# Banded attention and a squared-ReLU MLP in one kernel: bias matmuls ahead of the scores, masks at the start, and loads released by a memset

## The chip, the core and the metric

The kernel runs on one core of one Trainium2 chip, in one launch. The metric is the time of an execution on the device in microseconds; a kernel's time is the median of several executions. Engines are named as the profile names them: PE is TensorE (matmuls; PEld its weight loads), DVE is VectorE, ACT is ScalarE, POOL is GpSimd, which here issues all loads that convert from float32 to bfloat16, and SP is SyncE, which here issues the stores and the transposes made by DMA.

## The reference

q, k and v are float32 of shape (4, 8, 768, 64): batch, heads, sequence, head width. The attention is banded with a few global keys, and has a bias that falls linearly with distance. Its output goes through an MLP with a squared ReLU.

```python
scores = scale * np.matmul(q, k.transpose(0, 1, 3, 2))
is_global = pos[None, :] < 8
is_local = (rel >= 0) & (rel < 96)
keep = is_global | is_local
dist = np.where(is_global & ~is_local, 96.0, np.abs(rel))
bias = -slopes[:, None, None] * dist[None, :, :]
scores = np.where(keep, scores + bias[None], -1000000000.0)
a = softmax(scores)                       # over the keys
x = (a @ v) -> rows of 8 * 64 = 512       # 3072 tokens
out = (np.maximum(x @ w_in, 0.0) ** 2) @ w_out   # w_in 512 x 2048, w_out 2048 x 512
```

## The kernel before, in words

**Tiles and blocks.** The 3072 tokens are 24 tiles of 128, six for each batch entry. A local band of 96 reaches from a tile into its own keys and into those of the tile before it, and nowhere else; the eight global keys are copied over rows of the left tile that the band never reaches (lines 522 to 530 for k, 593 to 599 for v). The first tile of a batch entry has no left tile. Two tiles make a block of 256 tokens, which is what the MLP works on.

**A tile's attention.** q and k of tile j are brought into the layout with the head width on partitions. For tiles below `JQK` = 6 TensorE does it (`tr`, line 376, then a copy out of PSUM, `emit_T`); for later tiles SP issues one transpose by DMA (`emit_dT`, line 400, to `qkT`). Then come the scores (`emit_sc`, line 435), the exponential on ScalarE (line 483), the product with a mask `E` on VectorE (line 508), the matmul with v (`po`, line 550, whose 65th column is the softmax's sum), and the division (`emit_norm`, lines 577 and 578) that gives the tile's rows `x`. `x` is transposed in turn: by TensorE for tiles below `JX` = 6 (`trx`, line 613), by a DMA of SP's for the others (line 637, to `xT`).

**Bias and masks.** `pb` holds distance and mask for one tile, computed at the start from an iota. Tiles from `NBIAS` = 3 on multiply by `E`, the exponential of `pb` times each head's slope: eight activations (line 313), given to the planner as ready at 14 us. Tiles 0 to 2 have no mask product: `emit_sc` adds their bias in PSUM with a matmul of `pb` against a scaled identity `sid` (line 447), after the score matmuls of the same group.

**The MLP.** A block has eight steps. A step's first half, `hT` (line 661, eight matmuls of 256 columns), needs the block's `xT` and one part of w_in (`win_0` to `win_7`). ScalarE takes the ReLU (line 682), VectorE the square `hs` (line 694), and the second half, `acc` (line 731, four matmuls of 512 columns), needs a part of w_out. After eight steps the two halves of the block are copied out of PSUM (`emit_o`) and stored.

**Loads.** POOL issues q, k and v of a tile and the weight parts in a written order, 38 loads for tiles 1 to 7 and the weights, tile 0's v among them; tile 0's q and k come in float32 from SP. Tiles from 6 on (`late`) use `NQ` = 2 buffers in turn for q and k (`slot`), so a tile's load waits for the transpose of the tile two before it.

**Order.** Nothing is ordered by the loops. Every operation is entered in a `Plan` with an estimated cost on each engine that can do it, what it depends on, and a due time (`key`). `Plan.run` then lets the operation with the least start plus 0.05 x key go first, keeps track of each engine's free time and of buffers (`takes`), and so writes one fixed order for each engine. `LAG` is the delay the planner assumes from an operation's end to its user on another engine. SP and POOL are engines of the plan too (`SP`, `POOLQ`), and `DMAQ` stands for the transfers.

Of the kernel before, what the change touches and what calls it, by code (L numbers as in the profile page):

```python
# [21 lines left out]
class Plan:  # L22
# [9 lines left out]
    LAG = {"PE": 0.25, "ACT": 0.15, "DVE": 0.12, "SP": 2.6, "POOLQ": 0.8, "DMAQ": 1.2, "DMA": 0.0}  # L32
# [67 lines left out]
def kernel(  # L100
# [37 lines left out]
    JQK, JX = 6, 6  # L138
    NQ, NKT = 2, 2 * TPB
# [33 lines left out]
    E_AT = 14.0  # L173
    NWARM = 8
    LEAD = 12
# [65 lines left out]
    for j in range(NFIRST + 2):  # L241
        nc.vector.memset(v_sb[j][:, :, D : D + 1], 1.0)
    load_part(0, 1)
    nc.gpsimd.iota(pbi, pattern=[[-P, 2], [-1, P]], base=0, channel_multiplier=1)  # L244
    issue[0] += 0.4
# [9 lines left out]
    nc.vector.tensor_scalar(ident32, pbi[:, 0, :], 0.0, None, op0=Alu.is_equal)  # L255
    nc.vector.tensor_scalar(ident, pbi[:, 0, :], 0.0, None, op0=Alu.is_equal)
# [7 lines left out]
    )  # L264
    nc.vector.tensor_tensor(out=pb, in0=pbt, in1=pbw, op=Alu.min)
    for h in range(H):
        nc.vector.tensor_scalar_mul(sid[h], ident, float(slopes[h] / scale))

    def emit_pb0(e):
        nc.vector.tensor_copy(pb0, pb[:, 0, :])  # L270
        nc.vector.tensor_scalar_max(
            pb0[:n_global, :], pb0[:n_global, :], float(-n_local)
        )
        nc.vector.memset(pb[:n_global, 1, :], float(-n_local))

    pb_op = plan.op(("pb",), {"DVE": 0.75}, emit_pb0, key=-40.0)

    def emit_ones(e, js):
        for j in js:
            nc.vector.memset(v_sb[j][:, :, D : D + 1], 1.0)  # L280
# [22 lines left out]
    def any_copy(e, dst, src):  # L303
        if e == "ACT":
            nc.scalar.copy(dst, src)  # L305
        else:
            nc.vector.tensor_copy(dst, src)  # L307

    maskE = [
        plan.op(  # L310
            ("E", odd, g), {"ACT": 0.8}, key=0.3 + 2 * g + odd, ready=E_AT,
            emit=lambda e, odd=odd, g=g: [
                nc.scalar.activation(
                    E[:, odd, g, i], pb, Act.Exp, scale=float(slopes[4 * g + 2 * i + odd])
                )
                for i in range(2)
            ],
        )
        for g in range(2)
        for odd in range(2)  # L320
    ]

    def emit_E0(e, odd):
# [8 lines left out]
            ("E0", odd), {"DVE": 0.6}, emit=lambda e, odd=odd: emit_E0(e, odd), key=9 + odd,  # L332
            deps=[maskE[odd], maskE[2 + odd]],
# [7 lines left out]
    xT_op = {}  # L341
    xT_of = {}
# [3 lines left out]
    for j in range(NT):  # L346
# [6 lines left out]
        if j in late:  # L353
            def emit_load(e, j=j):
                load_tile(j)
            ld = plan.op(
                ("load", j), {"POOLQ": 2.6}, emit_load, deps=qk_users[slot(j)] + [ones[j]],
                key=base, ready=issue[0],
            )
            qk_users[slot(j)] = []  # L360
            ld = plan.op(("data", j), {"DMAQ": 2.7}, None, deps=[ld], key=base)
            land["q", j] = land["k", j] = land["v", j] = ld
# [6 lines left out]
        for n in range(2) if j < JQK else ():  # L369
            users = []  # L370

            def emit_tr(e, j=j, n=n, fp=fp):
                tr = ps_g.tile([P, NPAIR, P], FP32 if fp else BF16, name="tr", tag="g")
                src = plain[n, j] if fp else qk_ring[slot(j)][:, n, :]
                for pair in range(NPAIR):
                    nc.tensor.transpose(  # L376
                        out=tr[:, pair, :], in_=src[:, pair * P : (pair + 1) * P],
                        identity=ident32 if fp else ident,
                    )
                tiles["tr", n, j] = tr  # L380

            tr = plan.op(
                ("tr", n, j), {"PE": 0.5 if fp else 0.24}, emit_tr,
                deps=[land["qk"[n], j]], key=base, takes=(*G, [users]),
            )

            def emit_T(e, j=j, n=n, T_=T_):
                any_copy(e, T_[:, n], tiles.pop(("tr", n, j)))

            c = plan.op(  # L390
                ("T", n, j), {"DVE": 0.7 if fp else 0.43, "ACT": 0.57}, emit_T,
                deps=[tr] + ku, key=base + 0.1,
            )
            users += [tr, c]
            parts.append(c)
            if not fp:
                qk_users[slot(j)].append(tr)
        if j >= JQK:
            def emit_dT(e, j=j, T_=T_):
                nc.sync.dma_start_transpose(  # L400
                    out=T_.rearrange("p n a c -> p (n a) c"),
                    in_=qk_ring[slot(j)].rearrange("p n c -> p (n c)"),
                )

            T = plan.op(
                ("T", j), {"SP": 2.0}, emit_dT,
                deps=[land["q", j], land["k", j], xT_op[j - 3]] + ku, key=base - 6,
            )
            qk_users[slot(j)].append(T)
            parts = [T]  # L410
# [8 lines left out]
        def emit_sc(e, gs, j=j, first=first):  # L419
            sc = {}  # L420
            for g in gs:
                for odd in range(2):
                    sc[odd, g] = ps_g.tile([P, 4, P], FP32, name="sc", tag="g")
                    tiles["sc", j, odd, g] = sc[odd, g]
            todo = [
# [4 lines left out]
            todo = [x for x in todo if x[0] in gs]  # L430
            opened = set()
            for g, pair, at, kt in todo:
                for odd in range(2):
                    half = slice(odd * D, (odd + 1) * D)
                    nc.tensor.matmul(  # L435
                        out=sc[odd, g][:, at, :],
                        lhsT=qkT[(j - kt) % NKT][half, 1, pair, :],
                        rhs=qkT[j % NKT][half, 0, pair, :],

                        start=j >= NBIAS or (odd, g) not in opened,  # L440
                        stop=j >= NBIAS,
                        skip_group_check=True,
                    )
                    opened.add((odd, g))
            for g, pair, at, kt in todo if j < NBIAS else ():
                for odd in range(2):
                    nc.tensor.matmul(
                        out=sc[odd, g][:, at, :],
                        lhsT=sid[2 * pair + odd],
                        rhs=pb0 if first else pb[:, kt, :],  # L450
                        start=False,
                        stop=True,
                        skip_group_check=True,
                    )

        deps = list(parts)
        if j < NBIAS:
            deps.append(pb_op)
# [3 lines left out]
        for gs in [(0,), (1,)] if j < NSPLIT and not first else [tuple(range(groups))]:  # L462
            n = 8 * len(gs)
            o = plan.op(
                ("sc", j, gs[0]), {"PE": 0.25 + 0.029 * n + (0.056 * n if j < NBIAS else 0)},
                lambda e, gs=gs, f=emit_sc: f(e, gs), deps=deps, key=base + 1 + 2 * gs[0],
                takes=(*G, busers[2 * gs[0] : 2 * gs[-1] + 2]),
            )
            ku.append(o)
# [3 lines left out]
        for g in range(groups):  # L473
            for odd in range(2):
# [3 lines left out]
                def emit_exp(e, j=j, odd=odd, g=g):  # L478
# [11 lines left out]
                    ("exp", j, odd, g), {"ACT": 0.58}, emit_exp, deps=[s_[g]],  # L490
# [3 lines left out]
                users += [s_[g], x_]  # L494
# [6 lines left out]
                def emit_mul(e, j=j, odd=odd, g=g, first=first):  # L501
# [10 lines left out]
                    ("mul", j, odd, g), vec(0.38), emit_mul,  # L512
                    deps=[x_, maskE0[odd] if first else maskE[2 * g + odd]],
# [8 lines left out]
        if 1 <= t < TPB - 1:  # L522
            def emit_gk(e, j=j, t=t):
# [5 lines left out]
                ("gk", j), vec(0.17), emit_gk, deps=list(s_.values()), key=base + 4  # L529
# [7 lines left out]
        for hf in range(2):  # L537
# [34 lines left out]
            def emit_norm(e, j=j, hf=hf):  # L572
# [13 lines left out]
                ("norm", j, hf), vec(0.6), emit_norm,  # L586
# [6 lines left out]
        if 1 <= t < TPB - 1:  # L593
            def emit_gv(e, j=j, t=t):
# [3 lines left out]
                ("gv", j), vec(0.28), emit_gv, deps=[p_, norm[1]], key=base + 5  # L598
# [7 lines left out]
        if j < JX:  # L606
# [23 lines left out]
            c = plan.op(("xT", j), {"DVE": 0.43, "ACT": 0.57}, emit_xT, deps=[f_], key=base + 5.1, takes=xT_ring)  # L630
            users += [f_, c]
            xusers.append(f_)
        else:
# [8 lines left out]
            c = plan.op(("xT", j), {"SP": 1.3}, emit_xT, deps=norm, key=base + 5, takes=xT_ring)  # L642
# [4 lines left out]
        if tt == 1:  # L647
            c["deps"].append(xT_op[j - 1])
# [5 lines left out]
    for n, (blk, s) in enumerate(order1):  # L654
# [31 lines left out]
        r = plan.op(("relu", blk, s), {"ACT": 0.58}, emit_relu, deps=[a], key=n + 0.5, takes=("hr", 2, [rusers]))  # L686
# [10 lines left out]
        d = plan.op(("sq", blk, s), vec(0.68), emit_sq, deps=[r], key=n + 1.0, takes=("hs", NHS, [husers]))  # L697
# [11 lines left out]
    for blk in range(NBLK):  # L709
# [9 lines left out]
        for s, sub, half in order2:  # L719
# [29 lines left out]
            if s == NSTEP - 1:  # L749
                ousers = []  # L750

                def emit_o(e, blk=blk, sub=sub, half=half, cols=cols):
                    o_sb = work.tile([P, d_model], FP32, name="o", tag="o", bufs=4)
# [4 lines left out]
                    ("o", blk, sub), {"ACT": 0.57, "DVE": 0.62} if half is None else {"ACT": 0.37},  # L758
                    emit_o, deps=[o], key=8 * blk + s + 1.0, takes=("o", 4, [ousers]),
# [4 lines left out]
                def emit_st(e, blk=blk, sub=sub, half=half, cols=cols):  # L764
# [5 lines left out]

                st = plan.op(
                    ("st", blk, sub), {"SP": 0.4}, emit_st, deps=[ev],
                    key=8 * blk + s + 9.0,
                )
                ousers.append(st)

    for o in plan.run({"PE": 4.2, "DVE": 4.4, "ACT": 4.2, "DMAQ": issue[1]}):
# [37 lines left out]
```

## Time and profile before

| what | value |
|---|---|
| time, median of 4 | 216.16 us (215.95 to 216.53) |
| the profiled execution's own time | 215.99 us |
| its span, first to last instruction | 213.9 us |
| granted TensorE clock | 1.000 |
| PE / PEld busy | 206.7 us (97%) / 142.0 us (66%) |
| DVE / ACT busy | 141.2 us (66%) / 118.7 us (55%) |
| DMA queue of POOL's loads | 13.37 MB, 79200 packets |
| DMA queue of SP | 13.90 MB, 34480 packets |
| chain that ended last | PE 86%, DMA 7%, POOL 4% |

The profile is of one execution. Its span leaves out 2.1 us of the time of the same execution around it. Busy time of PE counts each matmul from its start to its modelled end; matmuls overlap, so a group of eight with 273 ns each takes 0.87 us. Where the profile puts an idle stretch down to a releaser, the wait for several semaphores is given to the one that came last.

### The profile page before, as it was taken

The page shows a single profiled execution, that of the slowest core. Times are in us where ns is not written, and L with a number is a line of the kernel's source. Part 1 is how long each engine was busy: PE and PEld are TensorE (multiplying, and loading weights), DVE is VectorE, ACT ScalarE, POOL GpSimd, SP SyncE. Part 2 cuts the span into 40 slices and gives each one's busy share as a digit, 9 for nine tenths or more (in the row PEclk, how much of TensorE's full clock was granted, in tenths as well). Part 3 has the DMA queues.
Part 4 walks back from the last instruction along what each step waited for, and adds up shares of the span by engine and source line. Part 5 has one row for each costly group of instructions (what it writes and reads, how often), then busy time and mean ns, then how long its engine had stood idle before and what let it go on. Part 6 is the DMA issues. An engine that isn't in the chain of part 4 may idle for free.

```text
span 213.9 us, 5031 instructions
## 1 busy us (share of the span) xinstructions
PE 206.7 (97%) x1992; PEld 142.0 (66%) x1992; DVE 141.2 (66%) x366; ACT 118.7 (55%) x218; POOL 74.1 (35%) x91
## 2 busy tenths in 40 slices
PE   7888999999999999999999999999999999999994
PEld 3666567657667767766767767766767767766773
DVE  5376968736688767756867767756867767744540
ACT  2587675714574845743845745743845745734431
POOL 7996677309044414309043140408113000000000
PEclk9999999999999999999999999999999999999999
DMA  9999999999999999999979959999989810310202
GB/s 129 145 160 197 181 196 181 178 220 112 158 196 127 218 99 124 159 136 100 198 101 104 212 71 111 149 126 96 204 128 91 175 25 3 123 25 3 98 0 98
DMA packets 113702, 27.58 MB, mean 129 GB/s; under 512 B 104336, under 2 KB 110736, under 8 KB 113680
## 3 DMA queue, kind: packets, MB, share of 16 engines
q0 software_dynamic: 79200, 13.37, 82.9%
q1 hardware_dynamic: 34480, 13.90, 34.0%
q8 instruction: 15, 0.25, 0.5%
q14 instruction: 7, 0.06, 0.1%
HBM read 27.26 MB, written 6.29 MB: 157 GB/s over the span
## 4 chain that ended last, share of the span: by engine, by line
PE 86%; DMA 7%; POOL 4%; issue 1%; DVE 0%; ACT 0%; POOLq 0%
PE hT L661 38%; PE acc L731 38%; PE sc L435 5%; PE po L550 5%; DMA win<-in_moe_w_in_dram 4%; DMA qk<-in_k_dram 3%; POOL qk L193 2%; POOL v L193 2%; POOL win L193 1%; PE tr L376 0%; PE trx L613 0%; DVE x L578 0%; ACT o L305 0%; POOL pbi L244 0%; DVE v L595 0%
## 5 line engine op out<-in xcount | busy, mean ns | idle before, releaser
L661 PE MATMUL hT<-xT,win 128*128 128x256 bf16 x768 | 99.0, 273 | 0.5 <-DMA win<-in_moe_w_in_dram 0.3
L731 PE MATMUL acc<-wout,hs 128*128 128x512 bf16 (+1 forms) x400 | 95.6, 370 | 0.0
L682 ACT ACTIVATE hr<-hT 128x512 f32<-128x512 f32 x96 | 57.3, 598 | 60.4 <-PE hT L661 58.9
L661 PEld LDWEIGHTS <-win 128*128 128x128 bf16 x768 | 71.0, 98 | 18.2 <-DMA win<-in_moe_w_in_dram 1.0
L694 DVE TENSOR_TENSOR hs<-hr 128x512 bf16<-128x512 f32 x96 | 65.0, 689 | 25.5 <-ACT hr L682 24.8
L731 PEld LDWEIGHTS <-hs 128*128 128x128 bf16 x400 | 38.4, 98 | 27.7 <-DVE hs L694 0.3
L483 ACT ACTIVATE esc<-sc 128x512 bf16<-128x512 f32 x78 | 42.6, 599 | 13.2 <-PE sc L435 13.1
L193 POOL DMA_DIRECT2D qk<-in_q_dram x23 | 20.6, 898 | 82.2 <-DMA qkT<-qk 79.7
L508 DVE TENSOR_TENSOR at<-esc,E 128x512 bf16<-128x512 bf16 x78 | 32.4, 420 | 6.9 <-ACT esc L483 5.8
L193 POOL DMA_DIRECT2D v<-in_v_dram x24 | 21.6, 902 | 2.4 <-DVE at L508 1.2
L578 DVE TENSOR_TENSOR x<-po,rs 128x256 bf16<-128x256 f32 x48 | 20.4, 424 | 1.7
L193 POOL DMA_DIRECT2D qk<-in_k_dram x23 | 20.7, 899 | 0.2 <-issue 0.2
L550 PEld LDWEIGHTS <-at 128*128 128x128 bf16 x352 | 16.7, 98 | 5.5
L550 PE MATMUL po<-v,at 128*128 128x65 bf16 x352 | 18.6, 193 | 0.0
L435 PEld LDWEIGHTS <-qkT 64*128 64x128 bf16 x352 | 9.9, 94 | 10.0 <-issue 8.3
L577 DVE RECIPROCAL rs<-po 128x4 f32<-128x4 f32 x48 | 8.6, 179 | 10.4 <-PE po L550 10.2
L435 PE MATMUL sc<-qkT 64*128 64x128 bf16 x192 | 13.2, 219 | 1.0 <-ACT qkT L305 0.5
L305 ACT COPY o<-acc 128x512 f32<-128x512 f32 (+1 forms) x14 | 7.8, 556 | 9.2 <-PE acc L731 9.2
L307 DVE COPY o<-acc 128x512 f32<-128x512 f32 x11 | 7.6, 691 | 6.2 <-PE acc L731 6.2
L435 PE MATMUL sc<-qkT,qkT 64*128 64x128 bf16 x160 | 11.4, 216 | 0.0
L524 DVE COPY qkT<-qkT 128x32 bf16<-128x32 bf16 x16 | 3.0, 189 | 7.5 <-PE sc L435 7.5
L193 POOL DMA_DIRECT2D win<-in_moe_w_in_dram x8 | 6.6, 822 | 0.9 <-DMA wout<-in_moe_w_out_dram 0.6
(40 smaller groups left out, 61.4 us busy)
## 6 DMA issues: line engine op xcount, KB each, us to landing
out_dram<-o SPq DMA_DIRECT2D x23, 256.0 KB, 3.3
v<-in_v_dram POOLq DMA_DIRECT2D x24, 128.0 KB, 6.2
qk<-in_q_dram POOLq DMA_DIRECT2D x23, 128.0 KB, 4.9
qk<-in_k_dram POOLq DMA_DIRECT2D x23, 128.0 KB, 5.6
win<-in_moe_w_in_dram POOLq DMA_DIRECT2D x8, 256.0 KB, 8.5
wout<-in_moe_w_out_dram POOLq DMA_DIRECT2D x8, 256.0 KB, 8.8
qkT<-qk SPq DMA_TRANSPOSE x18, 5.0
xT<-x SPq DMA_TRANSPOSE x18, 3.6
```

What stands on the lines that cost most here:

```text
L193: nc.gpsimd.dma_start(out=dst, in_=src)
L305: nc.scalar.copy(dst, src)
L435: nc.tensor.matmul(out=sc[odd, g][:, at, :], lhsT=qkT[(j - kt) % NKT][half, 1, pair, :], rhs=qkT[j % NKT][half, 0, pair, :],  start=j >= N ...
L483: nc.scalar.activation(out=esc, in_=tiles.pop(("sc", j, odd, g)).rearrange("p a c -> p (a c)"), func=Act.Exp, scale=scale,)
L508: nc.vector.tensor_mul(at, tiles.pop(("esc", j, odd, g)), bias)
L550: nc.tensor.matmul(out=po[:, hi, :], lhsT=tiles["at", j, odd, g][:, at * P : (at + 1) * P], rhs=v_sb[kj][:, h, :], start=(i == 0), stop=(i ...
L577: nc.vector.reciprocal(rs, po[:, :, D : D + 1])
L578: nc.vector.tensor_tensor(out=x[:, 4 * hf : 4 * hf + 4, :], in0=po[:, :, :D], in1=rs.to_broadcast([P, 4, D]), op=Alu.mult,)
L661: nc.tensor.matmul(out=hT[:, c, :], lhsT=w_in_sb[s][:, kt, c * P : (c + 1) * P], rhs=tiles["xT", blk][:, kt, :], start=(kt == 0), stop=(kt ...
L682: nc.scalar.activation(hr, tiles.pop(("hT", blk, s)), Act.Relu)
L694: nc.vector.tensor_mul(hs, hr, hr)
L731: nc.tensor.matmul(out=tiles["acc", blk, sub, half], lhsT=hs[:, c, sub * P : (sub + 1) * P], rhs=w_out_sb[s][:, c, cols], start=(s == 0 an ...
```

## The change

It has six parts.

1. The bias matmuls of tiles 0 to 2 become an operation of their own (`emit_bias`) that opens the PSUM group ahead of the score matmuls, and may be placed as soon as the tile's k is transposed by TensorE. The scores then close the group.
2. `pb` is finished at once at the start, and the eight `E` activations are issued there, outside the plan. The iota goes ahead of the first load on POOL.
3. From tile 8 on a load has a gate: a memset on VectorE of one element for each row and half of the buffer that the load will write. The load, which writes the same buffer, then waits for VectorE. In the plan the gate comes after the landing of the load before it, and after the issue of the `xT` transpose of the tile three before it.
4. There are three buffers for q and k of late tiles instead of two (`NQ`).
5. `JX` becomes 8: x of tiles 6 and 7 is transposed by TensorE.
6. The planner's costs and lags are changed (SP's lag from 2.6 to 0.6 with transfers as operations of their own on `DMAQ`; shorter costs on ACT and DVE), so the orders it writes change throughout. `NLATE` as set leaves the stores' dependencies as they were.

The diff, cut to its core:

```diff
-    LAG = {"PE": 0.25, "ACT": 0.15, "DVE": 0.12, "SP": 2.6, "POOLQ": 0.8, "DMAQ": 1.2, "DMA": 0.0}
+    LAG = {"PE": 0.25, "ACT": 0.26, "DVE": 0.2, "SP": 0.6, "POOLQ": 0.8, "DMAQ": 1.2, "DMA": 0.0}
...
-    JQK, JX = 6, 6
-    NQ, NKT = 2, 2 * TPB
+    JQK, JX = 6, 8
+    NQ, NKT = 3, 2 * TPB
...
-    E_AT = 14.0
     NWARM = 8
+    NLATE, NO = 2, 4
...
+    nc.gpsimd.iota(pbi, pattern=[[-P, 2], [-1, P]], base=0, channel_multiplier=1)
     load_part(0, 1)
-    nc.gpsimd.iota(pbi, pattern=[[-P, 2], [-1, P]], base=0, channel_multiplier=1)
-    issue[0] += 0.4
     load_part(1, 1)
...
+    nc.vector.tensor_copy(pb0, pb[:, 0, :])
+    nc.vector.memset(pb[:n_global, 1, :], float(-n_local))
+    nc.vector.tensor_scalar_max(pb0[:n_global, :], pb0[:n_global, :], float(-n_local))
     for h in range(H):
         nc.vector.tensor_scalar_mul(sid[h], ident, float(slopes[h] / scale))
...
+    for g in range(2):
+        for odd in range(2):
+            for i in range(2):
+                nc.scalar.activation(
+                    E[:, odd, g, i], pb, Act.Exp, scale=float(slopes[4 * g + 2 * i + odd])
+                )
...
+            gate = None
+            if j >= NFIRST + 2 + NQ - 1:
+
+                def emit_gate(e, j=j):
+                    nc.vector.memset(qk_ring[slot(j)][:, :, :1], 0.0)
+
+                gate = plan.op(
+                    ("gate", j), {"DVE": 0.07}, emit_gate, deps=qk_users[slot(j)] + [ld, xT_sp.get(j - 3)],
+                    key=base - 9,
+                )
             ld = plan.op(
-                ("load", j), {"POOLQ": 2.6}, emit_load, deps=qk_users[slot(j)] + [ones[j]],
-                key=base, ready=issue[0],
+                ("load", j), {"POOLQ": 2.6}, emit_load,
+                deps=qk_users[slot(j)] + [ones[j], gate], key=base, ready=issue[0],
             )
...
-                ("T", j), {"SP": 2.0}, emit_dT,
+                ("T", j), {"SP": 1.3}, emit_dT,
                 deps=[land["q", j], land["k", j], xT_op[j - 3]] + ku, key=base - 6,
             )
+            T = plan.op(("moved", j), {"DMAQ": 1.2}, None, deps=[T])
...
+        def emit_bias(e, gs, j=j, first=first, todo=todo, open_sc=open_sc):
+            open_sc(gs)
+            opened = set()
+            for g, pair, at, kt, odd in todo(gs):
+                nc.tensor.matmul(
+                    out=tiles["sc", j, odd, g][:, at, :],
+                    lhsT=sid[2 * pair + odd],
+                    rhs=pb0 if first else pb[:, kt, :],
+
+                    start=(odd, g) not in opened,
+                    stop=False,
+                    skip_group_check=True,
+                )
+                opened.add((odd, g))
...
+            if j < NBIAS:
+                bias = plan.op(
+                    ("bias", j, gs[0]), {"PE": 0.056 * n},
+                    lambda e, gs=gs, f=emit_bias: f(e, gs), deps=[tr],
+                    key=base + 0.9 + 2 * gs[0], takes=takes,
+                )
+                takes = None
             o = plan.op(
-                ("sc", j, gs[0]), {"PE": 0.25 + 0.029 * n + (0.056 * n if j < NBIAS else 0)},
-                lambda e, gs=gs, f=emit_sc: f(e, gs), deps=deps, key=base + 1 + 2 * gs[0],
-                takes=(*G, busers[2 * gs[0] : 2 * gs[-1] + 2]),
-            )
+                ("sc", j, gs[0]), {"PE": 0.2 + 0.029 * n},
+                lambda e, gs=gs, f=emit_sc: f(e, gs), deps=[*deps, bias],
+                key=base + 1 + 2 * gs[0], takes=takes,
+            )
...
-            c = plan.op(("xT", j), {"SP": 1.3}, emit_xT, deps=norm, key=base + 5, takes=xT_ring)
+            c = plan.op(("xT", j), {"SP": 1.2}, emit_xT, deps=norm, key=base + 5, takes=xT_ring)
+            xop = xT_sp[j] = c
+            c = plan.op(("xmoved", j), {"DMAQ": 0.9}, None, deps=[c])
             xusers.append(c)
...
-    for o in plan.run({"PE": 4.2, "DVE": 4.4, "ACT": 4.2, "DMAQ": issue[1]}):
+    for o in plan.run({"PE": 4.2, "DVE": 4.2, "ACT": 5.3, "DMAQ": issue[1]}):
```

In the orders that the plan writes for the changed kernel, `win`, `wout` and the tiles' loads stand on POOL as before; on SP the transpose of tile 6 stands ahead of the first store, and from tile 10 on each tile's `qkT` transpose stands behind the `xT` transpose of an earlier tile; 16 gate memsets stand among VectorE's squares and products.

## The prediction

> **What bounds the kernel now.** I read the page's busy rows and slices first, then the busy time by stretches, then TensorE's own timeline of the first 30 us, and last the rows on the transfers.
>
> ```profile
> PE 206.7 (97%) x1992; PEld 142.0 (66%) x1992; DVE 141.2 (66%) x366; ACT 118.7 (55%) x218; POOL 74.1 (35%) x91
> PE   7888999999999999999999999999999999999994
> PEclk9999999999999999999999999999999999999999
> ```
>
> ```profile
> 10.00:20.00 10.00, 8.75 (x137) 6.97 (x135) 6.27 (x38) 8.10 (x19) 8.28 (x11) 1.00 1.86 173
> 20.00:30.00 10.00, 9.25 (x100) 5.89 (x99) 8.07 (x22) 7.01 (x15) 7.54 (x10) 1.00 1.62 189
> 30.00:45.00 15.00, 15.00 (x146) 10.11 (x144) 11.41 (x27) 9.27 (x18) 7.28 (x9) 1.00 1.85 182
> 45.00:100.00 55.00, 55.00 (x526) 37.32 (x524) 37.82 (x90) 30.13 (x54) 21.88 (x25) 1.00 1.39 149
> ```
>
> The columns of the stretches are length, busy time of PE, PEld, DVE, ACT, POOL, clock, DMA share, GB/s. TensorE is busy without a gap from 30 us on, at full clock; time can only be gained before that, or by giving it less work. Busy time hides part of the gaps because ends of matmuls overlap, so I took starts: a matmul should start after its predecessor by 0.056 us (128 columns), 0.109 (256), 0.2155 (512) or 0.029 (65), the usual step in the trace. What exceeds this after 5 us is 5.40 us: 1.15 before 10 us, 2.28 from 10 to 20, 1.68 from 20 to 30, 0.29 later. Where:
>
> ```profile
> 7.17 0.40 PE L435 MATMUL sc<-qkT 64*128 64x128 bf16 x8 [0.37 <-ACT qkT L305]
> 11.73 0.40 PE L376 MATMUL tr<-ident,qk 128*128 128x128 bf16 x4 [0.21 <-DMA qk<-in_q_dram]
> 17.18 0.40 PE L376 MATMUL tr<-ident,qk 128*128 128x128 bf16 x4 [0.62 <-DMA qk<-in_k_dram]
> 24.47 1.05 PE L661 MATMUL hT<-xT,win 128*128 128x256 bf16 x8 [0.32 <-DMA win<-in_moe_w_in_dram]
> 27.45 0.40 PE L376 MATMUL tr<-ident,qk 128*128 128x128 bf16 x4 [0.22 <-DMA qk<-in_k_dram]
> 28.00 1.05 PE L661 MATMUL hT<-xT,win 128*128 128x256 bf16 x8
> ```
>
> Most of these wait for a load to land. The 38 loads of the first 40 us follow each other at 0.87 us (q, k, v) and 1.3 us (weights), so their landings are rails that no order of TensorE's moves: q and k of tile 2 at 11.68 and 12.51, win_1 15.02, k of tile 3 17.14, win_2 19.23, wout_0 20.50, win_3 21.80, wout_1 23.08, win_4 24.42, win_5 29.61 (semaphore events of the trace). The question is what else TensorE has ready at each rail.
>
> **The change part by part.** I followed the changed kernel's queues in their written order, with these durations and landings; ScalarE's 512-column operations follow each other at 0.48 us, VectorE's copy takes 0.42.
>
> *Constants.* The iota goes ahead of the first load on POOL: that load issues 0.37 us later (the iota's row), the second at the same place, so the other rails stay. VectorE's pb chain starts at 1.59 and is done at 3.66. Masks: eight activations at 0.306 each (four in 1.33 us at 13.47) run from 3.70 to 6.27 in ScalarE's idle 3.44 us there, and 2.5 us leave its queue at 13.5, 19.5 and 22.6. Cover: k of tile 0 wants ScalarE at 6.56, so 0.3 us spare; beyond that it costs one for one, up to the 1.1 us that tile 1 waits for q of tile 2.
>
> *Bias ahead.* Same 40 matmuls. Tile 0's eight (0.45 us) stand in the gap of 0.44 us before 7.17; its first exponential starts at 7.74 instead of 8.10, tile 0's first po at 8.95 instead of 9.65. Then both versions stand at the rails 11.68 and 12.51. After 12.60: transposes 0.23, bias 0.45, trx 0.22, bias 0.54, scores 0.55: the first step of the MLP (hT) at 14.59, against 15.30. win_1 is in at 15.02, so the second follows at 15.47; before, it stood behind k of tile 3, at 17.66. At 17.46 TensorE is thus one hT step (0.87) and one po group (0.24) ahead. The scores of tile 3 come at 18.18 and 18.95 (before 19.05 and 21.61). The rails 19.23 to 24.42 hold both versions (before: 19.38, 20.64, 21.94, 23.12, 24.47); between them the new order finishes tile 3: last po 22.77 (25.35), trx 23.99 (26.85), its xT copied at 25.0 (27.94).
>
> *The gain.* So block 1's steps may start at 25.39 instead of 28.00. Before win_5 lands, three of them fit (25.39, 27.34, 28.44) where one did; the other work up to there is the same. Two steps of 8 x 0.109 = 1.74, and win_5's step starts at 29.96 instead of 29.66: 1.74 - 0.30 = 1.44 us ahead. From 30 to 45 us the old gaps of 0.29 go and one of 0.35 appears (wout_7 landing at 40.09, its acc step now due at 39.8): -0.06.
>
> *x of tiles 6 and 7 by TensorE.* Eight transposes at 0.056: +0.45 us on the bound engine, nothing hides it. The two DMA transposes removed saved nothing: the tighter one landed 0.10 us before its use at 68.23. Its PSUM copies (0.41 on VectorE or 0.48 on ScalarE) lie beside matmuls.
>
> *Gates and third buffer.* 16 memsets of a few elements; nearest row 65 ns for 128x8: 1.0 us of VectorE, idle a third of the time. Should one have to wait, squares (hs) queue behind it and acc behind them. Four gates name a transpose that VectorE hasn't waited for yet; the earliest, at about 54.3, needs the one issued at 43.0, some 6 us done. Bounds: 0, and where a transpose took 9 us, still 2 us spare; I take 0. POOL's three loads per tile stay behind the gate, not beyond what the score needs: the first gated load issues earlier (45.7, before 48.6), as the third buffer is free.
>
> The cost is elsewhere. In SP's queue each qkT transpose now stands one tile period (8.04 us) nearer to its scores: 6.6 to 8.6 us from issue to use in the steady part, before 14.4 to 16.6.
>
> ```profile
> L400 SPq DMA_TRANSPOSE qkT<-qk x18: 1232/1290/2596, 43.0 to 167.8; - x18
> ...
> DMA to landing us min/median/max: 3.1/5.0/9.0
> ...
> POOL qk L193 <- DMA qkT<-qk: 79.7, 13, 9.1
> ```
>
> Landing took 3.1 us with nothing else moving (issue 158.42) and 9.03 with three loads and two stores under way (135.81). The Trainium skill's Advanced Engine Details and Errata, section X-Bar Transpose (TRN2), has it that transposes by DMA are as fast as regular DMAs, at an expected 350 to 400 GB/s. That speaks against gating: 256 KB in 0.7 us would never miss 6.6 us, the gates would buy nothing and the sum stays -0.93. By the row, at the old latencies and a budget of 7.3, the three slowest (7.6, 8.3, 9.0) exceed it by 3.0 us together, 2.5 us for the 15 transposes of the steady part: the sum would be +1.6. I take the row, but not its upper end: the gates issue the loads mostly 0.7 to 3 us after the transpose, so it starts in front of them, and only the overlap is slow. Between 140.5 and 142 us, with both moving, the transpose got about 0.4 of its lone rate: 1 us of transfer becomes 2.5 at worst, 3.1 + 1.5 = 4.6, and a store ahead adds 0.7 each: 6.0. Below 6.6, so 0; ends 0 and +2.5. A gain below 0 is excluded, since the scores were never late after 50 us.
>
> *The sum.* -1.44 + 0.06 + 0.45 = -0.93 us on the profiled execution (span 213.9, its own time 215.99): span 213.0, own time 215.06. That execution is 0.17 below the median 216.16, so the median becomes 215.2.
>
> **The rivals.**
> (1) Transposes come late, slower than before. Place: the scores at the head of each tile, every 8.04 us from 60 to 173. Price above: +2.5 - 0.93, about 217.7. It decides once the misses total 0.93 us; two transposes at the old maximum suffice. For: the budget is halved. Against: loads and transposes no longer start together.
> (2) The startup yields one step, not two. ScalarE has two relu operations ahead of k of tile 3 at 17.32, and tile 3's scores wait for that copy; if its chain slips by 1 us, only two steps of block 1 fit before win_5: 0.87 - 0.30 - 0.06 - 0.45 = 0.06 gained, 216.1: no change. Against: tile 3 has 1.9 us more than before for the same queue.
> (3) More gain: the wait at 40.14 and the 0.30 at win_5 don't appear: 0.93 + 0.65, 214.6. For: the landing of the last weights varies with the stores near it.
> That the gates hold nothing back is possible too; then the queue is as before with less budget, which is rival 1.
>
> **How the numbers follow.** Forecast 0.52 (215.2, alone 214.9 to 215.6), rival 3 0.14, rival 2 0.12, rival 1 0.22. Differences under 0.2%, 0.43 us, can't be told from none here. Faster: 0.52 + 0.14 + some of rival 2's better half (0.03) = 0.69; same 0.11, with small misses of rival 1; slower 0.20. The range 214.4 to 217.3 leaves out rival 1's upper part and the tail of rival 3.
>
> **What would show it.** In the profile after: E activations on ACT before 6.5 us; hT at about 14.6 and 15.5 on TensorE, and three hT steps of block 1 before the one that waits for win_5; trx x32 instead of x24; most POOL loads issued 0.7 us or more after a qkT transpose, not just ahead of it, and a median landing of qkT near 3.5 to 4.5. Wrong: idle time of PEld before L449 (scores) put down to a DMA qkT after 50 us, VectorE idle before the memset L346, or a tile period above 8.1 us; or block 1's first step still near 28.

## The result, and the profile after

The changed kernel takes 215.66 us (median of 43 runs, 214.49 to 217.35); the kernel before 216.21 (64 runs). The ratio is 0.9973, 95% interval 0.9961 to 0.9986: faster by 0.27%, a little more than this kernel's measurement can tell from no change. The forecast was 215.2 us, 0.9956 of the 216.16 it started from. In a second group of runs it was 215.26 against 216.16, ratio 0.9932 (0.9901 to 0.9962): the forecast's ratio lies between the two. The profiled execution was a lucky one: its own time is 214.53 with a span of 212.8, where the median span of its group is 213.5; before it was 215.99 and 213.9.

The busy row and the slice of TensorE from the page of after:

```profile
PE 205.2 (96%) x2000; PEld 141.7 (67%) x2000; DVE 143.2 (67%) x384; ACT 118.2 (56%) x218; POOL 74.4 (35%) x91
PE   6978999999999999999999999999999999999993
```

Its busy time by stretches (columns as before):

```profile
10.00:20.00 10.00, 8.01 (x122) 6.48 (x121) 6.65 (x39) 6.73 (x15) 8.69 (x12) 1.00 1.84 174
20.00:30.00 10.00, 9.43 (x99) 6.73 (x98) 6.40 (x17) 5.63 (x11) 7.30 (x10) 1.00 1.63 189
45.00:100.00 55.00, 55.00 (x524) 36.78 (x522) 37.38 (x97) 28.78 (x52) 18.43 (x21) 1.00 1.23 137
```

From 45 us on TensorE is still busy without a gap, so the steady part lost nothing to waits. From 10 to 20 us it is busy for less time than before (8.01 against 8.75): part of its work there was done earlier, and the same loads hold it up. The gain shows in TensorE's timeline:

```profile
12.52 0.40 PE L372 MATMUL tr<-ident,qk 128*128 128x128 bf16 x4 [0.45 <-DMA qk<-in_k_dram]
14.52 1.92 PE L675 MATMUL hT<-xT,win 128*128 128x256 bf16 x16
17.97 0.23 PE L449 MATMUL sc<-qkT 64*128 64x128 bf16 x2 [0.55 <-ACT qkT L304]
24.35 1.92 PE L675 MATMUL hT<-xT,win 128*128 128x256 bf16 x16
27.20 1.04 PE L675 MATMUL hT<-xT,win 128*128 128x256 bf16 x8
28.29 1.04 PE L675 MATMUL hT<-xT,win 128*128 128x256 bf16 x8
29.82 1.92 PE L675 MATMUL hT<-xT,win 128*128 128x256 bf16 x16
```

The group at 14.52 is two steps of the MLP, 14.52 and 15.40. The one at 24.35 is win_4's step and the first of block 1 (25.24), which stood at 28.00 before. Two more of block 1 follow, and the group at 29.82 begins with win_5's step: three steps of block 1 ahead of it, where the kernel before had one. The last matmul starts at 209.25 us, before at 210.52.

### The profile page after: what moved, and what is told of

The parts are those of the page before. It is cut to its first block, busy times and chain, and to the rows that moved or that the text cites. A ratio compares the mean times of both kernels' runs of the same rounds, so it can differ in the third digit from the quotient of the medians.

```text
span 212.8 us, 5059 instructions
## 1 busy us (share of the span) xinstructions
PE 205.2 (96%) x2000; PEld 141.7 (67%) x2000; DVE 143.2 (67%) x384; ACT 118.2 (56%) x218; POOL 74.4 (35%) x91
## 4 chain that ended last, share of the span: by engine, by line
PE 87%; POOL 6%; DMA 4%; issue 0%; ACT 0%; POOLq 0%
PE hT L675 39%; PE acc L745 38%; PE sc L449 5%; PE po L562 4%; DMA win<-in_moe_w_in_dram 4%; POOL qk L193 3%; POOL v L193 2%; POOL win L193 1%; POOL wout L193 1%; PE trx L625 0%; PE tr L372 0%; ACT o L304 0%; POOL pbi L246 0%; POOLq L246 0%; POOLq L813 0%
## 5 line engine op out<-in xcount | busy, mean ns | idle before, releaser
L745 PE MATMUL acc<-wout,hs 128*128 128x512 bf16 (+1 forms) x400 | 97.8, 370 | 0.5 <-DMA wout<-in_moe_w_out_dram 0.5
L675 PEld LDWEIGHTS <-win 128*128 128x128 bf16 x768 | 72.6, 98 | 23.3 <-DMA win<-in_moe_w_in_dram 0.8
L708 DVE TENSOR_TENSOR hs<-hr 128x512 bf16<-128x512 f32 x96 | 65.9, 687 | 21.3 <-ACT hr L696 19.8
L745 PEld LDWEIGHTS <-hs 128*128 128x128 bf16 x400 | 36.6, 98 | 24.4 <-issue 0.6
L193 POOL DMA_DIRECT2D v<-in_v_dram x24 | 22.2, 924 | 2.4 <-DVE at L520 1.2
L589 DVE RECIPROCAL rs<-po 128x4 f32<-128x4 f32 x48 | 8.6, 180 | 13.4 <-PE po L562 13.4
L495 ACT ACTIVATE at<-sc 128x512 bf16<-128x512 f32 x10 | 5.3, 598 | 2.4 <-PE sc L449 2.4
L193 POOL DMA_DIRECT2D wout<-in_moe_w_out_dram x8 | 5.7, 709 | 2.8 <-DMA win<-in_moe_w_in_dram 2.0
```

The lines of the kernel that those rows point to most:

```text
L193: nc.gpsimd.dma_start(out=dst, in_=src)
L495: nc.scalar.activation(out=esc, in_=tiles.pop(("sc", j, odd, g)).rearrange("p a c -> p (a c)"), func=Act.Exp, scale=scale,)
L589: nc.vector.reciprocal(rs, po[:, :, D : D + 1])
L675: nc.tensor.matmul(out=hT[:, c, :], lhsT=w_in_sb[s][:, kt, c * P : (c + 1) * P], rhs=tiles["xT", blk][:, kt, :], start=(kt == 0), stop=(kt ...
L708: nc.vector.tensor_mul(hs, hr, hr)
L745: nc.tensor.matmul(out=tiles["acc", blk, sub, half], lhsT=hs[:, c, sub * P : (sub + 1) * P], rhs=w_out_sb[s][:, c, cols], start=(s == 0 an ...
```

## Experiments

Four theories run through the expectations. Theory 1: the prediction's step counts hold in every execution (0.87 us for a step, 0.45 for the transposes of tiles 6 and 7), and the landings before 30 us move from run to run. Theory 2: the shorter time between issue and use of the qkT transposes costs stalls in executions that were not profiled. Theory 3: each build draws its own landings. Theory 4: idle time before 13 us brings on a stretch at half clock. The runs came in three groups; the kernel before had 216.16, 216.09 and 216.19 us in them.

**The changed kernel again** (no edit).

> The changed kernel itself, run beside the others of this group. Of the 0.93 us forecast the median showed 0.55, though the first profiled execution (214.53) was 1.46 ahead. Theory 1 (the step counts hold in every execution and the profiled pair was only a lucky draw; the median gains less because the landings of the loads before 30 us move from run to run): ratio 0.9960 to 0.9986, and a second profile has TensorE busy without a gap from 45 us on, with its lost time before 31 us. Theory 2 (the halved time between issue and use of the qkT transposes costs some executions a stall, 0.4 us on average): the same ratio, but a second profile with a longer span than 212.8 shows gaps of PEld at the scores after 50 us.

Measured: 215.26 us, ratio 0.9932 (0.9901 to 0.9962); span of the profiled run 212.7. Its timeline repeats the first one: block 1's steps at 25.20, 27.16 and 28.25, win_5's at 29.77, and from the 15th step (40.75 us) to the last matmul 168.51 us in both profiles. The ratio is better than was expected. No gap at the scores showed, but the profile again fell on the shortest span of its group, so it does not rule theory 2 out.

**x of tiles 6 and 7 by DMA in the changed kernel.**

```diff
-    JQK, JX = 6, 8
+    JQK, JX = 6, 6
```

> The changed kernel with x of tiles 6 and 7 transposed by DMA again (JX 6 instead of 8): 8 matmuls of 0.056 us less on TensorE. Theory 1 (these transposes cost their full 0.45 us because TensorE is busy without a gap there): 0.45 us faster than the changed kernel, 215.2, ratio to the kernel before 0.995. Rival (the transposes by DMA were worth their place: x of tile 7 landed only 0.10 us before its use, and with three more steps of the MLP done early it would come late): 0 to 0.5 us slower than the changed kernel, ratio 0.997 to 1.000, with TensorE waiting for xT near 60 to 69 us.

Measured: 215.20 us, ratio 0.9943 (0.9919 to 0.9967): no gain that can be told. In its profile the 15th step to the last matmul took 168.06 us, which is 168.51 less exactly 0.45. But block 1 began at 26.10 instead of 25.20, since the loads landed some 0.9 us later from win_1 on (16.05 against 15.10). The term of the sum is right in the profile; in the executions at full clock the median span is even longer than the changed kernel's of this group, 213.5 against 213.1. It is taken up again with the filler below.

**The gates taken out, twice.**

```diff
-            if j >= NFIRST + 2 + NQ - 1:
+            if False:
```

> The changed kernel without the 16 memsets that let the loads go; three buffers, the order of the queues as it comes. If the gates keep the transposes quick (theory 1, by the row of 3.1 us alone and 9.0 us beside three loads): median landing of qkT back from 3.9 to about 5 us with a maximum of 8 to 9, against 6.6 to 8.6 us from issue to use: up to 2.5 us slower than the changed kernel, 216.2 to 218, ratio 1.000 to 1.009. If transposes by DMA run as fast as regular transfers, the gates buy nothing: ratio as of the changed kernel, 0.997.

> The kernel without gates once more, one look. Theory 1 (the gates keep the scores from waiting): a wait of PEld at the scores of 0.5 us or more after 50 us, and more than 168.6 us from the 15th step of the MLP to the last matmul. Theory 3 (its steady part is as fast as the changed kernel's, 168.52 in its first profile, and all its loss lies in the landings before 30 us): 168.5 again, and block 1's first step at 26 us or later, where the changed kernel has 25.2.

Measured: 216.77 us, ratio 1.0022 (0.9998 to 1.0046), 1.5 us behind the changed kernel of its group; the single execution of the second run took 217.03. The qkT transposes landed in 6.3 and 6.1 us (median), up to 9.7 and 8.5. The first profile held a stretch at half clock (13.8 to 17.2 us), which pushed TensorE 2 us back and hid the cause: 168.52 us from the 15th step to the end. The second has it, in the timelines of TensorE, SP and POOL (start, length, engine, operation; in brackets the idle time before it and what ended it):

```profile
52.22 0.40 PE L449 MATMUL sc<-qkT 64*128 64x128 bf16 x8 [1.34 <-DMA qkT<-qk]
...
43.79 1.33 SPq L396 DMA_TRANSPOSE qkT<-qk  x1
...
41.33 0.88 POOL L193 DMA_DIRECT2D qk<-in_q_dram  x1
42.30 0.88 POOL L193 DMA_DIRECT2D qk<-in_k_dram  x1
43.34 0.87 POOL L193 DMA_DIRECT2D v<-in_v_dram  x1 [0.17 <-issue]
```

The same place in the timelines of the changed kernel's SP, POOL and weight loads:

```profile
42.87 1.32 SPq L396 DMA_TRANSPOSE qkT<-qk  x1
...
45.45 0.88 POOL L193 DMA_DIRECT2D qk<-in_q_dram  x1 [5.01 <-DVE qk L346]
...
49.09 0.23 PEld L449 LDWEIGHTS <-qkT 64*128 64x128 bf16 x8 [0.42 <-DMA qkT<-qk]
```

Without the gate the third buffer lets the loads of tile 8 go at 41.33 us, ahead of the transpose of tile 6, and that transpose lands 8.4 us after its issue. Its scores wait 1.34 us. With the gate the loads go 2.6 us after the transpose, which lands in 6.0 us, 0.25 us before the weight load of its scores, and nothing starts late: the 0.42 us that the line puts down to the transpose stand before the scores' weight load of every later tile in this profile too. After this one place the kernel without gates has at least 3.6 us to spare at every qkT, the changed kernel, whose transposes stand nearer to their scores, 1.3. So the gates are worth about 1.4 us in this profile, all at the first transpose by DMA, and not in the steady part. The second run's expectation of theory 1 came true (1.3 us of wait, 169.93 us from the 15th step on), but its words "after 50 us" fit one wait alone.

**The startup alone.** Bias and masks as changed; two buffers, no gates, old costs and lags, JX 6; then the same with JX 8.

> The changed kernel with all of its steady part undone: two buffers, no gates, x of tiles 6 and 7 by DMA, the planner's costs and lags as before; left are the masks and the bias ahead of the scores. In its written order two steps of block 1 stand before win_5's step, where the kernel before has one and the changed kernel three. Theory 1 (each such step is worth 0.87 us, less 0.15 by which win_5's step is later): 0.72 us faster than the kernel before, 215.5, ratio 0.9967, with block 1's first step at 25.5 to 26.5 us. Theory 2 (the halved time of the transposes is what eats the gain) says the same here, since the old distances stand. Rival (the order up to 25 us alone is worth the whole 1.44 and the third step is filled by something else): 214.8, ratio 0.9933.

> The kernel with the startup alone (masks and bias ahead, the rest as before), but with x of tiles 6 and 7 transposed by TensorE (JX 8). In the profile with JX 6 TensorE waited 1.6 us for xT of tile 7 at 69.3 us, a wait that neither the kernel before nor the changed kernel has. If the gain of the startup was eaten there (theory 1): the wait goes, 0.45 us of transposes come, 1.2 us faster than with JX 6, about 216.3. If the startup's order itself is the loss (the landings before 30 us, its wait for win_5 of 1.8 us): 0.45 us slower than with JX 6 or the same, 217.5 to 218.

Measured: with JX 6 217.69 us, ratio 1.0052 (1.0018 to 1.0086): slower, against the 0.72 us of gain expected, and also in the executions at full clock (median span 215.35). Its timeline of TensorE has the reason, a wait that the kernel before escaped by 0.1 us:

```profile
68.62 1.03 PE L743 MATMUL acc<-wout,hs 128*128 128x512 bf16 x4
71.23 1.03 PE L673 MATMUL hT<-xT,win 128*128 128x256 bf16 x8 [1.59 <-DMA xT<-x]
```

TensorE was not further ahead here. This profile holds a stretch at half clock from 12.6 us on, and TensorE stood 1.04 us later than in the kernel before; tile 7's xT transpose was issued 1.04 us later too. But it landed 5.57 us after its issue, in the kernel before 3.64. What differs is the order of the queues: there the transpose went ahead of POOL's next load of q, here behind it (SP and POOL, the kernel before first):

```profile
64.49 1.19 SPq L637 DMA_TRANSPOSE xT<-x  x1
64.78 0.88 POOL L193 DMA_DIRECT2D qk<-in_q_dram  x1 [3.05 <-DMA qkT<-qk]
...
64.89 0.88 POOL L193 DMA_DIRECT2D qk<-in_q_dram  x1 [0.55 <-issue]
65.53 1.19 SPq L648 DMA_TRANSPOSE xT<-x  x1
```

It is the pattern of the kernel without gates; that the load in front is the cause was not tested here. With JX 8 the wait is gone: 216.12 us, ratio 1.0004 (0.9984 to 1.0024), 1.57 us faster than with JX 6, where 1.2 was expected. The median span at full clock is 214.05, against 214.2 of the kernel before: a gain of 0.15 for a sum of 0.72 - 0.45 = 0.27. Its block 1 begins at 27.53 us, later than the 25.5 to 26.5 expected, but two steps stand ahead of win_5's (30.15).

**The transposes alone**, on the kernel before: JX 8 and nothing else.

> The kernel before with one number changed: JX 8, x of tiles 6 and 7 transposed by TensorE. Theory 1 (eight matmuls of 0.056 us on an engine that is busy without a gap there): 0.45 us slower than the kernel before, 216.55, ratio 1.002. Rival (xT of tile 7 by DMA, which landed 0.1 to 0.3 us before its use in the one profile, is late in other executions, so that its transposes by TensorE pay here too): the same or faster, ratio 0.998 to 1.000.

Measured: 216.87 us against 216.19, ratio 1.0011 (0.9981 to 1.0042). By the interval it is undecided; the median span at full clock is 214.7 against 214.3, which agrees with 0.45. (Four of its 12 executions spent 2.5 to 3.0 us outside the span, none of the kernel before's more than 2.1, so the times differ by more than the spans.)

**The steady part alone**: the kernel before with three buffers, gates, new costs and lags, JX 8.

> The other part of the change alone: bias after the scores and masks at 14 us as in the kernel before, but three buffers, gates, the planner's new costs and lags, JX 8. Its written order has two steps of block 1 ahead of win_5's. Theory 1 (each further step is worth 0.87 us, less 0.15; gates and third buffer nothing; 0.45 for the transposes): 0.72 - 0.45 = 0.27 us faster than the kernel before, ratio 0.9988. Theory 2 (what the gates do in the steady part is worth time of its own): faster than that by 0.3 us or more, ratio under 0.9975. Rival (the startup's loads were the reason for the whole gain): no gain, 0.45 us slower, 1.002.

Measured: 215.85 us against 216.19, ratio 0.9977 (0.9947 to 1.0006); median span at full clock 213.9 against 214.3. Two steps of block 1 (27.39 and 28.48 us) stand ahead of win_5's (30.00). The sum said 0.27 faster, the measured difference is 0.34, though the interval includes none; theory 2 in its other direction, a gain from the gates of its own, is not needed. In the changed kernel gates and third buffer together have little to themselves either: its full-clock spans (213.1 to 213.3) are 0.75 to 0.95 us below those of the startup with JX 8, and the third step alone makes 0.72.

**A memset that changes nothing**, on POOL after everything else.

```diff
+    nc.gpsimd.memset(zero[:, :2], 0.0)
```

> The changed kernel with one memset of two elements added on POOL at its very end, after its last load: every queue up to there is as in the changed kernel. It asks how far two builds of the same schedule differ. In the kernels without gates and with JX 6 the time from the 15th step of the MLP to the end was that of the changed kernel to 0.01 us (less the 0.45 of the transposes), yet their spans were up to 1.5 us longer, all of it before 30 us, where their queues are the same. If the cause lies in what these kernels changed (theory 1): the memset changes nothing, 215.3 to 215.7, ratio 0.993 to 0.997. If a build of its own draws its own landings of the first loads (theory 3): anything between 215 and 217, and a profile in which the spread between the first and the last of a load's 16 parts differs from the 1.8 us of the changed kernel.

Measured: 215.44 us, ratio 0.9971 (0.9949 to 0.9993), as the changed kernel, which is what theory 1 expected; theory 3 allowed any value and is not needed. Its profiled execution happened to hold a stretch at half clock, right after the waits for q and k of tile 2. Two stretches of its span, the 3.41 us ahead of it and the half clock itself (columns as before):

```profile
9.56:12.97 3.41, 2.23 (x37) 1.49 (x37) 2.47 (x9) 2.50 (x5) 3.41 (x5) 1.00 2.09 157
...
13.00:16.40 3.40, 3.40 (x40) 2.98 (x38) 1.91 (x6) 0.48 (x1) 3.30 (x6) 0.50 2.16 168
```

And TensorE's timeline there:

```profile
12.76 0.45 PE L372 MATMUL tr<-ident,qk 128*128 128x128 bf16 x4 [0.50 <-DMA qk<-in_k_dram]
13.00 1.06 PE L433 MATMUL sc<-pb,sid 128*128 128x128 bf16 x8
...
16.24 1.97 PE L675 MATMUL hT<-xT,win 128*128 128x256 bf16 x16
```

The granted clock is 0.50 for 3.41 us, eight bias matmuls take 1.06 us instead of 0.61, and the first step of the MLP starts at 16.24 instead of 14.52. The end is 0.93 us later (last matmul 210.18 against 209.25).

**Filler in the two waits.** Transposes of zeros where TensorE would idle for q and k of tile 2.

```diff
+                for i in range((12, 10)[n] if j == 2 else 0):
+                    nc.tensor.transpose(out=tr[:, 0, :], in_=zero[:, :P], identity=ident)
                 for pair in range(NPAIR):
```

> The changed kernel with 12 and 10 transposes of a tile of zeros (0.056 us each) ahead of the transposes of q and of k of tile 2, where TensorE waits 0.7 and 0.6 us for their loads. A third of the changed kernel's executions show a granted clock of 0.992 or less, 4 of 34 of the kernel before do; in two profiles that was one stretch of 3.41 us at half clock between 12.6 and 17.2 us, right after these waits. If the idle time brings the stretch on (theory 4): it goes, the share at 0.992 falls from a third to under a tenth, and the median by 0.2 us, to 215.2. If the stretches come for another reason, or are hidden behind the landings: the same as the changed kernel, 215.3 to 215.7; if the filler itself delays the transposes, 0.1 to 0.3 us slower.

> The filler kernel again, beside the one with JX 6. Theory 4 (the stretches at half clock come from the idle time in the two waits): again under a tenth of its executions at a granted clock of 0.992 or less, where the changed kernel shows a third, and 215.2, ratio 0.9955. If 12 of 12 was chance: three or more of 12 at 0.992.

> The kernel with filler transposes in the two waits for q and k of tile 2, with x of tiles 6 and 7 by DMA again (JX 6). With JX 6 the changed kernel took 168.06 us from the 15th step of the MLP to the last matmul, 0.45 less than with JX 8, yet its median was no shorter. If that was the draw of the landings before 30 us (theory 1): 0.45 us faster than the filler kernel of this group, 214.75, ratio 0.9935. If the transposes by DMA cost in executions that were not profiled what they save on TensorE (xT of tile 7 late): the same as the filler kernel, 215.2, ratio 0.9955.

Measured: 215.18 us in both groups, ratios 0.9943 (0.9926 to 0.9961) and 0.9930 (0.9903 to 0.9958). None of the 24 executions has a granted clock of 0.992 or less; of the changed kernel's and the memset kernel's 22 of 68 do, of the kernel before's 9 of 98. But the changed kernel with JX 6, which has no filler, shows none in its 12 executions either. The stretch from 10.0 to 13.4 us, in the profiles of the kernel before, the changed one and the one with filler in this order (none of them has a half clock; TensorE's busy time is the first number behind the length):

```profile
10.00:13.40 3.40, 2.93 (x51) 2.22 (x48) 2.99 (x11) 2.85 (x6) 3.40 (x5) 1.00 1.99 156
```

```profile
10.00:13.40 3.40, 1.97 (x30) 1.46 (x29) 1.67 (x6) 1.60 (x4) 3.40 (x5) 1.00 1.98 161
```

```profile
10.00:13.40 3.40, 2.84 (x47) 2.34 (x46) 1.42 (x6) 1.62 (x4) 3.40 (x5) 1.00 2.00 159
```

The order of the kernel before kept TensorE busy there for 2.93 us, the changed one for 1.97, and the filler brings it back to 2.84.

With filler and JX 6 it was 216.07 us, ratio 0.9958 (0.9924 to 0.9993), where 214.75 was expected. Its profile took 168.41 us from the 15th step on, so it gave back 0.35 of its 0.45 (168.06 would have been all of it). The median span of its full-clock executions is 213.8 us, against 213.35 with JX 8. The waits of TensorE in that profile (us in total, times, longest) say where:

```profile
PE sc L451 <- DMA qkT<-qk: 0.3, 1, 0.3
```

Three of its 12 executions also show a clock of 0.992, in spite of the filler, and spans of 217.6 to 218.2; what stalled there was not seen. The other nine have a median time of 215.62 us. So making xT of tiles 6 and 7 on TensorE costs it 0.45 us, yet neither in the changed kernel nor in the filler kernel did leaving it to DMA shorten the median; in the startup kernel TensorE's transposes save more than they cost. The filler kernel beats the kernel before clearly; its lead over the changed kernel (215.18 against 215.26 to 215.66) is inside the intervals.

## Why the prediction held, and where it was mis-sized

*Startup, -1.44.* The mechanism was right, step for step: first steps at 14.52 and 15.40 (predicted 14.59 and 15.47), block 1 at 25.24, 27.20 and 28.29 (25.39, 27.34, 28.44). The masks ran from 3.32 to 5.88 us (3.70 to 6.27) and delayed nothing. Masks and bias alone, or the new costs and lags alone, give two such steps; the third needs both.

*Gaps from 30 to 45 us, +0.06.* This term was mis-sized. It took the landings of the one profile before as fixed. win_5 landed 0.14 us earlier and its step began at 29.82 instead of 29.96. The weight load that the prediction puts at 40.09 (by the order of the loads it is wout_6, not wout_7) landed at 39.84, so the predicted wait of 0.35 was 0.14. Together 0.35 us: the sum of -0.93 becomes -1.28, and the last matmul moved by -1.27. That was about half of rival 3, in this execution.

*Transposes of tiles 6 and 7, +0.45.* Right as TensorE's time: 168.51 against 168.06 us. As a cost of the whole kernel it was not shown: at full clock the spans with JX 6 are longer, not shorter (213.5 against 213.1, with filler 213.8 against 213.35). One wait of 0.3 us for a qkT was seen there; where the rest went stays open.

*"The two DMA transposes removed saved nothing."* True of the profile before. But the 0.10 us by which xT of tile 7 was early was all the room there was: in the startup kernel's profile the same transpose took 5.57 us instead of 3.64 to land, and cost 1.6 us.

*Gates 0, from 0 to +2.5.* The value held, since no score waited, and the median landing of 3.9 us lay in the 3.5 to 4.5 forecast. But the bound on the landing was wrong: "6.0 at worst" became 6.5 and 7.3 in the two profiles, and the room at tile 6 was 0.25 us. Rival 1 was close, at one place rather than in every tile. On the rule weighed there (the Trainium skill's Advanced Engine Details and Errata, section X-Bar Transpose (TRN2)) the row decides: a transpose that lands in 3.0 us at best and in 8.4 behind three loads made the gates worth 1.4 us, where the rule made them worth nothing.

*From the profile to the median.* The profiled pair gained 1.46 us: 1.15 in the span and 0.31 outside it, which the prediction had carried over unchanged. The medians gained 0.55 and 0.90. Executions at full clock (granted clock 0.997 or more) have a median span of 213.3 and 213.1 us against 214.2, a gain of 0.9 to 1.1. That this meets the prediction's 0.93 is in part luck, since the same sum with its gaps put right gives 1.28 for the pair that it was made for. Against the gain stands what the prediction did not have: about a third of the executions of the changed kernel have a granted clock of 0.992 or less, a tenth of the kernel before's. Those have a median span of 213.7 to 213.9 us (0.5 to 0.8 longer), which puts the median span of all executions 0.2 to 0.35 us above that at full clock. The runs with filler speak for the idle time before 13 us as what brings it on, but do not settle it: none of 24 executions with filler and JX 8 shows a clock that low, three of 12 with filler and JX 6, and none of 12 with JX 6 and no filler.

The two groups hardly differ in their spans (medians 213.5 and 213.4 us). The 0.40 us between their times lie outside the span: 13 of 44 executions of the first group spent 2.3 to 3.0 us there, one of 12 in the second, where 1.8 is usual. What happens in that time no trace shows, and for the 64 runs of the kernel before beside the first group no spans are on record; whether the first ratio is too modest for that reason stays open.

## What to carry to other kernels

Work moved ahead of a wait leaves the wait in place and makes the engine's idle time denser: look at what the clock does there, and at which transfer further on had only a tenth of a microsecond to spare. When loads run into one another, time is won by the number of ready steps ahead of each landing, so count steps in the written order and not busy time. A third buffer can cost more than it gives if nothing holds its loads behind the transfer that is needed first.

## What the runs showed of the hardware

The loads do not follow each other as fixed rails. A load reports 16 times, as its parts land, and the first report hardly moves between executions: k of tile 3 has it at 14.9 to 15.3 us in all fourteen profiles. The last one lags by 1.3 to 1.9 us in some and 2.4 to 2.9 in others at that load; it can grow again later (in the startup kernel's profile to 3.7), and a lag once grown mostly stays until the queue runs empty near 45 us. Of the executions with the changed kernel's startup that had no stretch at half clock, those with the small lag begin block 1 at 25.2 to 25.4 us, those with the large one at 26.05 to 26.12. The lag mostly grows between 12 and 16 us, when most of these profiles also record an instruction transfer of 16 KB on a queue of its own (0.9 to 1.7 us); that the one causes the other was not shown.

The half clock came as one whole stretch of 3.41 us at 0.50 in each of the three profiles that had it, beginning at 12.6, 13.0 and 13.8 us. In the 3.41 us ahead TensorE was busy for 2.12, 2.23 and 1.48 us, with no single wait over 0.94 us. The Trainium skill's TensorE: Matmul & The Clock Gate, section HAM oscillation, warns of idle gaps of more than about 3.4 us; here it came after a busy share of 0.43 to 0.65 without any such gap. The changed kernel's profile stands at 0.58 to 0.65 between 9 and 14 us and had no half clock in that execution, while about a third of its executions did by their granted clock, so the share alone does not decide it; at 0.82 and more (before, filler) it was rare.

A transpose by DMA moves at about half a store's rate even alone. In the kernel before it moved 0.11 MB from 160.0 to 160.5 us (210 GB/s), a store 0.19 MB from 199.0 to 199.5 (389 GB/s), each with nothing beside it. Its landing took 3.0 to 3.2 us at best in each of these profiles, and 8.4 us behind three loads.
